# A long convolution by FFT on one Trainium2 core: the first transform stage with the tokens as the stationary operand, evicted by ScalarE

## Chip, cores and metric

The program runs on one core of a Trainium2 chip. The metric is device time in microseconds, the median of several executions. All data are float32. The engines that matter are TensorE (PE in the profile, with its weight loads in a row of their own, PEld), VectorE (DVE), ScalarE (ACT), GpSimd (POOL) and SyncE (SP), which only issues transfers here.

## The reference

Two blocks follow each other. The first convolves every channel of x with a filter as long as the sequence; the second is a soft mixture of experts, in which 32 slots are filled by a softmax over the tokens, pass through small two-layer networks, and are handed back to the tokens by a softmax over the slots.

```python
batch, seq, d_model = (8, 5696, 128)          # x, and h of (seq, d_model)
Xf = np.fft.rfft(x, n=2 * S, axis=1)
Hf = np.fft.rfft(h, n=2 * S, axis=0)
y = np.fft.irfft(Xf * Hf[None], n=2 * S, axis=1)[:, :S, :]
...
x = y.reshape(B * S, D)                       # 45568 x 128
logits = x @ phi                              # phi: 128 x 32
d = exp(logits - logits.max(0)); d /= d.sum(0) + 1e-9
slot_input = d.T @ x                          # 32 x 128
...                                           # 8 experts, 4 slots each
c = exp(logits - logits.max(1)); c /= c.sum(1) + 1e-9
out = c @ slot_out
```

## The kernel before

The transform of 5696 tokens is split into a first stage over 89 rows (90 frequencies, of which 45 pairs are kept) and a second over 64 columns, both as dense matrix products. The 128 channels are taken 64 at a time. I call the work on 64 channels of one sequence a **half**: halves 0 and 1 are the filter h, halves 2 to 17 are the eight sequences of x. `H` counts them.

- `load_x(H)` (L181, issues on L189) brings a half into `X[H % 2]`, 89 rows by 64 tokens by 64 channels, by eight transfers on SP's queue. Two buffers.
- `fold(H, j)` (L192, instructions on L202), j = 0 to 3, on GpSimd: 32 sums and 32 differences of mirrored tokens, written over X. Each j makes a quarter of both, so a product of the first stage needs all four.
- `stage_a(H, k)` (L205), the first stage. The cosine and sine tables `s1` are stationary (89 x 32), X is moving (32 tokens x 16 channels, 512 columns). Eight products fill two PSUM banks `pa`, in which the frequencies lie on the partitions. A VectorE transpose of 32 x 32 blocks (L224) then puts the tokens on the partitions, in `F1` or `F3`. Six such units make a half: four of 64 slots, two of the 26 slots that are left over. `pa` has one buffer, F1 and F3 too.
- `stage_b1(n)` (L231), the second stage (PE, L249, into PSUM `bt`, one buffer), and four VectorE operations: two products with the filter's spectrum (L277; L272 where the form doesn't allow one operation) and two sums (L291). For halves 0 and 1 the products are with phase tables, in four operations, and the sums are the filter's spectrum.
- `stage_b2(n)` (L296): the inverse of the second stage (PE, L310 and L321), a ScalarE eviction (L325, L330) to `zst`, and a transfer to DRAM (`z`, L331, SP's queue).

The main loop (L587) runs over **steps** n; H and i are n divided by 6 and its remainder, and each half takes six steps. In step n the order is: `stage_b1(n)` with its two products, one `stage_a` unit (none at i = 0), the sums, `stage_b2(n - 1)`, a second `stage_a` unit (only at i = 5), `load_x(H + 2)` at i = 3, then a third of the rest of the pipeline, called **C** here, and at i = 5, 0, 1, 2 one `fold`. The unit at i = 3 is the first of half H + 1.

C works from step 26 on, on a quarter of a sequence at a time (32 in all), three steps each. At i = 2 and 5: `stage_c3` (logits), `dispatch` and the first two inverse products of `stage_c1` (PE, L379, from `zc`). At i = 0 and 3: `stage_c6`, `column_max`, `stage_c4` (with the GpSimd subtraction on L460), the last two products of `stage_c1` (L379), their VectorE folds (L385, L386), four GpSimd additions and subtractions (L401), and `load_pair` (L351), which brings the next `zc` from DRAM over SP's queue. At i = 1 and 4: `stage_c5`, `softmax` (GpSimd product on L480) and `stage_c2`, PE transposes of what L401 wrote (L410). `zc` has one buffer here. Where a new sequence begins, `load_pair` runs at i = 1, because the last `z` block must be written first.

The schedule is manual: on each engine the instructions stand in the order in which the code issues them.

Of the kernel before, what the change touches and what calls it, by code (L numbers as in the profile page):

```python
# [23 lines left out]
def slots_of_tail(NG):  # L24

    ks = np.zeros(NG, dtype=int)
    for s in range(NG):
        o, par = divmod(s, 2)
        ks[s] = 2 * (2 * (o // 2) + par) + o % 2 if o < NG // 2 - 1 else NG - 2 + par
    return ks  # L30


def transform_tables(S, N1, N2, CH):

# [4 lines left out]
    NG = N1 - 64  # L39
# [5 lines left out]
    kg = 64 + slots_of_tail(NG)  # L45
    s1 = np.zeros((P, 3, 3, 32))
    s1[:R1, :, 0] = part[:, :, 0:64:2]
    s1[:R1, :, 1] = part[:, :, 1:64:2]
    s1[:R1, :, 2, :NG] = part[:, :, kg]
# [14 lines left out]
    wt = np.zeros((2, N2, 32, N2))  # L64
    wg = np.zeros((2, N2, NG, N2))
    vt = np.zeros((2, N2, 2, 16, N2))
    vg = np.zeros((2, N2, NG // 2, N2))
    t1 = np.zeros((2, N2, 2, 4, 2, 4))
    t3 = np.zeros((2, N2, 2, NG // 2))
    for a in range(2):  # L70
        for s in range(32):
            k = 2 * s + a
            wt[a, :, s] = fore[k]
            o, par = divmod(s, 2)
            vt[par, :, a, o] = w[k][back].T
            t1[par, :, :, o // 4, a, o % 4] = cs[:, k].T
        for s in range(NG):
            wg[a, :, s] = fore[kg[s]]
    for s in range(NG):
        o, par = divmod(s, 2)  # L80
        vg[par, :, o] = w[kg[s]][back].T
        t3[par, :, :, o] = cs[:, kg[s]].T
    wt, wg, vt, vg, t1, t3 = [t.reshape(P, *t.shape[2:]) for t in (wt, wg, vt, vg, t1, t3)]
    return [np.ascontiguousarray(t, dtype=np.float32) for t in (s1, i1, wt, wg, vt, vg, t1, t3)]
# [3 lines left out]
def kernel(  # L88
# [29 lines left out]
    NG = N1 - 64  # L118
    HD = D // 2
    assert S == R1 * N2 and R1 == N1 - 1 and D == P and CH == Q == 4  # L120
# [3 lines left out]
    t_s1, t_i1, t_wt, t_wg, t_vt, t_vg, t_t1, t_t3 = [  # L124
        nc.inline_tensor(t, f"tab_{n}").ap()
        for n, t in zip(("s1", "i1", "wt", "wg", "vt", "vg", "t1", "t3"),
                        transform_tables(S, N1, N2, CH))]
# [35 lines left out]
    s1 = fconst.tile([P, 3, 3, 32], F32, name="s1")  # L163
    wt = fconst.tile([P, 32, N2], F32, name="wt")
    wg = fconst.tile([P, NG, N2], F32, name="wg")
    vt = fconst.tile([P, 2, 16, N2], F32, name="vt")
    vg = fconst.tile([P, NG // 2, N2], F32, name="vg")
    t1 = fconst.tile([P, 2, 4, 2, 4], F32, name="t1")
    t3 = fconst.tile([P, 2, NG // 2], F32, name="t3")
    H1 = [fconst.tile([P, 2, 4, 2, 4, HD], F32, name=f"H1{i}") for i in "ri"]  # L170
    H3A = [fconst.tile([P, 2, 2, 8, 32], F32, name=f"H3A{i}") for i in "ri"]
    H3B = [fconst.tile([P, 2, 2, 5, 32], F32, name=f"H3B{i}") for i in "ri"]
    F1 = bpool.tile([P, 32, 2, HD], F32, name="F1")
    F3 = bpool.tile([P, 32, 2, 32], F32, name="F3")
    X = [apool.tile([P, N2 + 8, HD], F32, name=f"X{i}") for i in range(2)]
# [5 lines left out]
    def load_x(H):  # L181

        if H >= NH:
            return
        g, dh = divmod(H, 2)
        src = (h if g == 0 else x[g - 1]).rearrange("(a n) d -> a n d", n=N2)
        for n0 in (0, 48, 16, 32):
            for r in (slice(0, SPLIT), slice(SPLIT, R1)):
                nc.sync.dma_start(out=X[dh][r, 8 + n0:24 + n0, :],  # L189
                                  in_=src[r, n0:n0 + 16, dh * HD:(dh + 1) * HD])  # L190

    def fold(H, j):  # L192


        if H >= NH:
            return
        t_ = X[H % 2]
        lo = 8 + 8 * j
        hi = 71 - 8 * j
        for op_, dst in ((AL.add, t_[0:R1, 8 * j:8 * j + 8, :]),  # L200
                         (AL.subtract, t_[0:R1, hi:hi - 8:-1, :])):
            nc.gpsimd.tensor_tensor(out=dst, in0=t_[0:R1, lo:lo + 8, :],  # L202
                                    in1=t_[0:R1, hi:hi - 8:-1, :], op=op_)

    def stage_a(H, k):  # L205


        if H >= NH:
            return lambda: None
        t_ = X[H % 2]  # L210
        p = aps.tile([P, 2, 512], F32, name="pa", tag="pa")
        for c in range(2):
            for q in range(4):
                a, comp = divmod(q, 2)
                d0 = 16 * k if k < 4 else 16 * (k - 4) + 32 * a
                nc.tensor.matmul(p[32 * q:32 * q + 32, c, :],  # L216
                                 s1[0:R1, comp + c, a if k < 4 else 2, :],
                                 t_[0:R1, 40 * comp:40 * comp + 32, d0:d0 + 16],
                                 start=True, stop=True)

        def turn():
            f_ = F1[:, :, :, 16 * k:16 * k + 16] if k < 4 else \
                F3[:, :, :, 16 * (k - 4):16 * (k - 4) + 16]
            nc.vector.transpose(f_.rearrange("p k c d -> p c d k"),  # L224
                                p[:, :, :].rearrange("p c (n d) -> p c d n", d=16))

        return turn
# [3 lines left out]
    def stage_b1(n):  # L231


        H, i = divmod(n, 6)
        g, dh = divmod(H, 2)
        bt = bps.tile([P, 2, 512], F32, name="bt", tag="bt")
        o0, no = (0, 4) if i < 4 else (0, 8) if i == 4 else (8, 5)
        for o in range(no):
            for a in range(2):
                r = slice(a * HP, (a + 1) * HP)  # L240
                for par in range(2):
                    if i < 4:
                        s = 8 * i + 2 * o + par
                        l_, m_ = wt[r, s, :], F1[r, s, :, :]
                    else:
                        s = 2 * (o0 + o) + par
                        l_, m_ = wg[r, s, :], F3[r, s, :, :]
                    w_ = 2 * (HD if i < 4 else 32)
                    nc.tensor.matmul(bt[par * HP:(par + 1) * HP, a, o * w_:(o + 1) * w_], l_,  # L249
                                     m_.rearrange("p c d -> p (c d)"), start=True, stop=True)  # L250
        dn = HD if i < 4 else 32
        pi = bpool.tile([P, 2, 512], F32, name="pi", tag="pi")
        y_ = bpool.tile([P, 1024], F32, name="y", tag="y", bufs=2) if g else None

        def split(t):
            return t[:, :, 0:no * 2 * dn].rearrange("p a (o c d) -> p a o c d", c=2, d=dn)

        pv, iv = split(bt), split(pi)
        Hs = [[H1, H3A, H3B][max(0, i - 3)][k][:, dh] for k in range(2)]
        if i < 4:  # L260
            Hs = [v[:, i] for v in Hs]
        if g:
            fs = [[v, v] for v in Hs]
        else:
            fs = [(t1[:, k, i] if i < 4 else
                   t3[:, k, o0:o0 + no].unsqueeze(1).broadcast_to([P, 2, no])).unsqueeze(3)
                  .broadcast_to([P, 2, no, dn]) for k in range(2)]
            fs = [[v, v] for v in fs]
        for dst, f_ in ((iv, fs[1]), (pv, fs[0])):
            if i == 5 or g == 0:  # L270
                for c in range(2):
                    nc.vector.tensor_tensor(out=dst[:, :, :, c, :], in0=pv[:, :, :, c, :],  # L272
                                            in1=f_[c], op=AL.mult)
            else:
                m = lambda v: v.rearrange("p a o c d -> p (a o) c d")
                w_ = f_[0].rearrange("p a o d -> p (a o) d").unsqueeze(2)
                nc.vector.tensor_tensor(out=m(dst), in0=m(pv), in1=w_.broadcast_to([P, 2 * no, 2, dn]),  # L277
                                        op=AL.mult)

        def sums():  # L280
            if g == 0:
                outs = [(0, AL.add, Hs[0]), (1, AL.subtract, Hs[1])]
            else:
                if i < 4:
                    yv = y_[:, :].rearrange("p (a o c d) -> p a o c d", a=2, c=2, d=dn)
                else:
                    yv = y_[:, 0:no * 128].rearrange("p (o c a d) -> p a o c d", c=2, a=2, d=dn)
                outs = [(1, AL.add, yv[:, :, :, 1, :]), (0, AL.subtract, yv[:, :, :, 0, :])]
                prods[n] = y_
            for c, op_, dst in outs:  # L290
                nc.vector.tensor_tensor(out=dst, in0=pv[:, :, :, c, :], in1=iv[:, :, :, 1 - c, :],  # L291
                                        op=op_)
# [3 lines left out]
    def stage_b2(n):  # L296
        H, i = divmod(n, 6)
# [4 lines left out]
        bz = bps.tile([P, 2, 512], F32, name="bz", tag="bz")  # L302
        st = bpool.tile([P, 4, 2, P], F32, name="zst", tag="zst", bufs=2)
        if i < 4:
            for o in range(4):
                for par in range(2):
# [559 lines left out]
```

## Time and profile before

| | |
|---|---|
| median of three runs | 1081.16 us (1080.51 to 1091.31) |
| the profiled execution's own time | 1075.27 us |
| its span | 1073.3 us |
| PE busy, share of the span | 828.1 us, 77% |
| DVE busy | 784.3 us, 73% |
| POOL busy | 408.1 us, 38% |
| ACT busy | 338.0 us, 31% |
| mean granted TensorE clock | 0.888 |

The times of this document are from the profiled execution unless it says otherwise. Groups of instructions are given with their line in the kernel, the tile written and the tiles read, the shape, the number of records and the mean duration of one. A float32 product leaves two records on PE, each with a weight load on PEld. The span falls into a start (to 51 us, the first `stage_b1`), four halves without C (to 254 us), the halves with C (to about 910 us) and a tail without any first stage.

### The profile page before, as it was taken

What the parts mean: (1) busy time and instruction counts of PE and PEld (TensorE: products, weight loads), DVE (VectorE), ACT (ScalarE), POOL (GpSimd) and SP (SyncE); (2) the same over time, 40 slices, a digit from 0 to 9 for tenths busy, and PEclk for the clock granted to TensorE, in tenths of its full rate; (3) what the DMA queues carried; (4) which work ended last, traced back from release to release, by engine and by line L of the source; (5) the groups of instructions that cost most, each with busy time, mean ns of one, the idle gap of its engine ahead of it and who ended that gap; (6) DMA issues with size and microseconds to landing.
All of it is one profiled execution on the core that took longest, in us unless ns stands there. A gap on an engine that the chain in (4) does not pass through costs nothing.

```text
span 1073.3 us, 28430 instructions
## 1 busy us (share of the span) xinstructions
PE 828.1 (77%) x12368; PEld 455.5 (42%) x12368; DVE 784.3 (73%) x1025; ACT 338.0 (31%) x661; POOL 408.1 (38%) x387
## 2 busy tenths in 40 slices
PE   0655557676888888887988888888888888896893
PEld 0122223343444444444544444444444445444683
DVE  1275656666878789888988888898888989484442
ACT  0000001111233334334343343343343434476432
POOL 3402120303234535464654535465453534275000
PEclk9975555867889999999999999999999999896865
DMA  9130301634758574868658384866758345965499
GB/s 228 18 53 3 55 1 40 127 88 108 158 165 166 145 177 126 186 147 210 129 173 191 121 196 132 212 121 192 163 150 177 118 150 186 310 221 226 154 381 340
DMA packets 222040, 167.55 MB, mean 156 GB/s; under 512 B 108438, under 2 KB 204182, under 8 KB 218774
## 3 DMA queue, kind: packets, MB, share of 16 engines
q1 hardware_dynamic: 220620, 162.04, 57.7%
q10 hardware_dynamic: 1296, 3.68, 1.1%
q8 instruction: 98, 1.61, 0.6%
q14 instruction: 26, 0.21, 0.1%
HBM read 90.30 MB, written 75.31 MB: 154 GB/s over the span
## 4 chain that ended last, share of the span: by engine, by line
PE 28%; DVE 26%; DMA 19%; POOL 10%; ACT 3%; issue 3%; SPq 2%; DVEq 0%; POOLq 0%; ACTq 0%
DMA zc<-z 15%; PE pa L216 9%; POOL y L401 8%; DVE F L224 6%; PE bank L379 6%; PE bt L249 6%; DVE y L291 4%; DMA out_dram<-o 4%; DVE pi L277 3%; DVE bt L277 3%; POOL L L460 2%; PE bank L410 2%; DVE y L385 2%; DVE y L386 2%; SPq L189 2%
## 5 line engine op out<-in xcount | busy, mean ns | idle before, releaser
L216 PE MATMUL pa<-X,s 89*32 89x512 f32 x1728 | 248.9, 698 | 51.8 <-POOL X L202 27.4
L224 DVE STREAM_TRANSPOSE F<-pa 128x1024 f32<-128x1024 f32 x108 | 212.2, 1965 | 81.5 <-PE pa L216 81.4
L325 ACT ACTIVATE zst<-bz 128x1024 f32<-128x1024 f32 x96 | 91.6, 955 | 547.7 <-PE bz L310 431.2
L202 POOL TENSOR_TENSOR X<-X 89x512 f32<-89x512 f32 x144 | 183.2, 1273 | 197.7 <-DMA X<-in_x_dram 173.0
L379 PE MATMUL bank<-zc,i 128*64 128x512 f32 x480 | 119.6, 618 | 42.8 <-DMA zc<-z 22.8
L249 PE MATMUL bt<-F,wt 64*64 64x128 f32 x2304 | 94.2, 310 | 56.1 <-DVE y L291 24.2
L249 PEld LDWEIGHTS bt<-F,wt 64*64 64x64 f32 x2304 | 74.4, 152 | 107.4 <-issue 70.0
L216 PEld LDWEIGHTS pa<-X,s 89*32 89x32 f32 x1728 | 49.9, 120 | 162.2 <-issue 94.4
L291 DVE TENSOR_TENSOR y<-bt,pi 128x512 f32<-128x512 f32 x192 | 115.5, 640 | 0.7
L451 POOL MEMSET dt<- 64x8 f32 x32 | 3.4, 108 | 267.2 <-issue 249.8
L277 DVE TENSOR_TENSOR pi<-bt,H1i 128x1024 f32<-128x1024 f32 x64 | 78.0, 1219 | 26.3 <-PE bt L249 26.3
L410 PE MATMUL bank<-ident,y 109*128 109x109 f32 x512 | 67.0, 267 | 33.7 <-ACT d L470 19.0
L401 POOL TENSOR_TENSOR y<-y,op 128x512 f32<-128x512 f32 x64 | 77.4, 1210 | 34.1 <-DVE op L385 31.5
L310 PEld LDWEIGHTS bz<-y,vt 64*64 64x64 f32 x2048 | 58.9, 139 | 56.8 <-issue 56.8
L277 DVE TENSOR_TENSOR bt<-bt,H1r 128x1024 f32<-128x1024 f32 x64 | 78.2, 1222 | 0.0
L310 PE MATMUL bz<-y,vt 64*64 64x128 f32 x2048 | 75.0, 287 | 0.0
L410 PEld LDWEIGHTS bank<-ident,y 109*128 109x128 f32 x512 | 52.5, 145 | 45.8 <-POOL y L401 38.9
L379 PEld LDWEIGHTS bank<-zc,i 128*64 128x64 f32 x480 | 30.5, 138 | 94.5 <-issue 39.0
L401 POOL TENSOR_TENSOR y<-y,om 128x512 f32<-128x512 f32 x56 | 66.7, 1191 | 2.2
L385 DVE TENSOR_TENSOR y<-bank,y 128x512 f32<-128x512 f32 x32 | 22.1, 689 | 60.8 <-PE bank L379 60.8
L249 PE MATMUL bt<-F,wg 64*64 64x64 f32 x1872 | 39.8, 238 | 24.9 <-DVE y L291 11.2
L412 ACT ACTIVATE yt<-bank 128x360 f32<-128x360 f32 x128 | 53.8, 476 | 16.4 <-PE bank L410 16.4
(109 smaller groups left out, 1041.1 us busy)
## 6 DMA issues: line engine op xcount, KB each, us to landing
z<-zst SPq DMA_DIRECT2D x80, 512.0 KB
zc<-z SPq DMA_DIRECT2D x30, 1024.0 KB
X<-in_x_dram SPq DMA_DIRECT2D x64, 320.0 KB
out_dram<-o SPq DMA_DIRECT2D x16, 1024.0 KB
zc<-z SPq DMA_DIRECT2D x30, 416.0 KB
out_dram<-o SPq DMA_DIRECT2D x8, 768.0 KB
z<-zst SPq DMA_DIRECT2D x16, 320.0 KB
c_t<-cst SPq DMA_DIRECT2D x26, 180.0 KB
```

What stands on the lines that cost most here:

```text
L202: nc.gpsimd.tensor_tensor(out=dst, in0=t_[0:R1, lo:lo + 8, :], in1=t_[0:R1, hi:hi - 8:-1, :], op=op_)
L216: nc.tensor.matmul(p[32 * q:32 * q + 32, c, :], s1[0:R1, comp + c, a if k < 4 else 2, :], t_[0:R1, 40 * comp:40 * comp + 32, d0:d0 + 16], ...
L224: nc.vector.transpose(f_.rearrange("p k c d -> p c d k"), p[:, :, :].rearrange("p c (n d) -> p c d n", d=16))
L249: nc.tensor.matmul(bt[par * HP:(par + 1) * HP, a, o * w_:(o + 1) * w_], l_, m_.rearrange("p c d -> p (c d)"), start=True, stop=True)
L277: nc.vector.tensor_tensor(out=m(dst), in0=m(pv), in1=w_.broadcast_to([P, 2 * no, 2, dn]), op=AL.mult)
L291: nc.vector.tensor_tensor(out=dst, in0=pv[:, :, :, c, :], in1=iv[:, :, :, 1 - c, :], op=op_)
L310: nc.tensor.matmul(bz[a * HP:(a + 1) * HP, par, o * P:(o + 1) * P], vt[r, a, 4 * i + o, :], y_[r, k * P:(k + 1) * P], start=True, stop=True)
L325: nc.scalar.activation(st[:, 0:no, :, :].rearrange("p o q x -> p q o x"), bz[:, :, 0:no * P].rearrange("p q (o x) -> p q o x", x=P), AF.Copy)
L379: nc.tensor.matmul(p[h_ * HP:(h_ + 1) * HP, :], i1[0:kr, tab, :], t_[0:kr, h_, o, :, :, q, :].rearrange("k n e d -> k (n e) d"), start=Tru ...
L401: eng.tensor_tensor(out=part_, in0=part(v, 0), in1=o_[:, :, :], op=sign)
L410: nc.tensor.transpose(p[:, i * TR:(i + 1) * TR], ys[T][0:TR, k * CH + i, 0:D], ident[0:TR, 0:TR])
L412: nc.scalar.activation(yt[:, k * CH:(k + 1) * CH, :, :], of_tokens(p), AF.Copy)
```

## The change

The first stage swaps its operands: 32 folded tokens of one channel become the stationary operand, and the tables are moving. Each product then leaves the tokens on the partitions directly. Four products (sums and differences, for even and odd frequencies) go to the four groups of 32 PSUM partitions; 16 channels make 64 products, and one ScalarE activation moves the unit to `Fs`. The 45 slots are cut into 24 and 21, so a half has eight units, l = 0, 1 and k = 0 to 3. Rows of X are padded from 64 to 66 channels. The leftover slots lose their own form: F1 and F3 become `Fs`, and stages b1 and b2 handle six blocks of slots in one way (five of eight slots, one of five).

```diff
-    s1 = fconst.tile([P, 3, 3, 32], F32, name="s1")
...
+    s1 = fconst.tile([P, 2, 2, 3, SL], F32, name="s1")
...
+    SL = 24
     HD = D // 2
+    XP = HD + 2
...
-    X = [apool.tile([P, N2 + 8, HD], F32, name=f"X{i}") for i in range(2)]
+    Fs = bpool.tile([P, NP, 2, HD], F32, name="Fs")
+    X = [apool.tile([P, N2 + 8, XP], F32, name=f"X{i}") for i in range(2)]
...
-    def stage_a(H, k):
...
-        p = aps.tile([P, 2, 512], F32, name="pa", tag="pa")
-        for c in range(2):
-            for q in range(4):
-                a, comp = divmod(q, 2)
-                d0 = 16 * k if k < 4 else 16 * (k - 4) + 32 * a
-                nc.tensor.matmul(p[32 * q:32 * q + 32, c, :],
-                                 s1[0:R1, comp + c, a if k < 4 else 2, :],
-                                 t_[0:R1, 40 * comp:40 * comp + 32, d0:d0 + 16],
-                                 start=True, stop=True)
-        def turn():
-            f_ = F1[:, :, :, 16 * k:16 * k + 16] if k < 4 else \
-                F3[:, :, :, 16 * (k - 4):16 * (k - 4) + 16]
-            nc.vector.transpose(f_.rearrange("p k c d -> p c d k"),
-                                p[:, :, :].rearrange("p c (n d) -> p c d n", d=16))
-        return turn
+    def stage_a(H, l, k):
         t_ = X[H % 2]
+        p = aps.tile([P, 16, HD], F32, name="pa", tag="pa")
+        s0, ns = l * SL, min(SL, NP - l * SL)
+        for d in range(16):
+            for q in range(4):
+                a, comp = divmod(q, 2)
+                nc.tensor.matmul(
+                    p[32 * q:32 * q + 32, d, 0:2 * ns].rearrange("p (c k) -> p c k", c=2),
+                    t_[0:R1, 40 * comp:40 * comp + 32, 16 * k + d],
+                    s1[0:R1, a, l, comp:comp + 2, 0:ns], start=True, stop=True)
+        nc.scalar.activation(
+            Fs[:, s0:s0 + ns, :, 16 * k:16 * k + 16],
+            p[:, :, 0:2 * ns].rearrange("p d (c k) -> p k c d", c=2), AF.Copy)
...
+    for k in range(4):
+        stage_a(0, 0, k)
+    stage_a(0, 1, 0)
     fold(1, 0)
-    for k in range(4):
-        stage_a(0, k)()
+    fold(1, 1)
...
-        turns = [(H + 1, 0)] if i == 3 else [(H + 1, 1)] if i == 4 else \
-            [(H + 1, 2), (H + 1, 3)] if i == 5 else [(H, 3 + i)] if i else []
+        turns = [(H, 1, i + 1)] if i < 3 else []
+        if i >= 2:
+            turns.append((H + 1, 0, i - 2))
+        if i == 5:
+            turns.append((H + 1, 1, 0))
...
-        if i in (5, 0, 1, 2):
-            fold(H + 2 if i == 5 else H + 1, (i + 1) % 6)
+        if i in (4, 5, 0, 1):
+            fold(H + 2 if i >= 4 else H + 1, (i + 2) % 6)
```

In a step the units now stand so: one at i = 0, 1, 3 and 4, two at i = 2 and i = 5, the second of them after `stage_b2`. The first unit of half H + 1 moves from i = 3 to the second place of i = 2, and each `fold` moves one step ahead. The tables and the filter's spectrum are laid out anew to fit; their loads at the start become fewer, of about the same size.

## The prediction

> **What bounds the kernel now.** I read the page first: the two busiest engines and the clock, in 40 slices of 26.8 us.
>
> ```profile
> PE   0655557676888888887988888888888888896893
> DVE  1275656666878789888988888898888989484442
> PEclk9975555867889999999999999999999999896865
> ```
>
> In the first quarter PE and DVE are half busy and the granted clock is low; from slice 12 on both are at eight tenths and the clock is full. Neither is a plain bound. Next the groups that the change touches:
>
> ```profile
> L216 PE MATMUL pa<-X,s 89*32 89x512 f32 x1728 | 248.9, 698 | 51.8 <-POOL X L202 27.4
> L224 DVE STREAM_TRANSPOSE F<-pa 128x1024 f32<-128x1024 f32 x108 | 212.2, 1965 | 81.5 <-PE pa L216 81.4
> ```
>
> The transposes are 212.2 us of DVE, all of which go. What that is worth is read from the order of time. Without C, the trace shows b1, a unit, its transpose, the sums and only then the next b1 (bt has one buffer): halves 0 to 3 start at 51.37, 103.76, 156.34 and 205.73 and end at 253.60, that is 52.4, 52.6, 49.4 and 47.9 us, with a unit at 3.64 us at the low clock and 1.92 at the full one. So there the transpose is on the path.
>
> With C it isn't. PE of one step i = 2 in the timeline (start, length), then GpSimd around it, then SP at the next i = 3:
>
> ```profile
> 604.90 1.10 PE L249 MATMUL bt<-F,wt 64*64 64x128 f32 x32
> 605.93 1.92 PE L216 MATMUL pa<-X,s 89*32 89x512 f32 x16
> 607.79 1.10 PE L310 MATMUL bz<-y,vt 64*64 64x128 f32 x32
> 608.82 0.81 PE L418 MATMUL bank<-yt,phi 128*32 128x360 f32 x8
> 609.45 1.07 PE L491 MATMUL bank<-y,d 128*32 128x129 f32 x32
> 610.86 2.02 PE L379 MATMUL bank<-zc,i 128*64 128x512 f32 x8 [0.34 <-ACT lt L424]
> ```
>
> ```profile
> 599.15 2.46 POOL L401 TENSOR_TENSOR y<-y,op 128x512 f32<-128x512 f32 x2
> 601.56 2.47 POOL L401 TENSOR_TENSOR y<-y,om 128x512 f32<-128x512 f32 x2
> 603.99 2.63 POOL L202 TENSOR_TENSOR X<-X 89x512 f32<-89x512 f32 x2
> 606.58 1.04 POOL L480 TENSOR_TENSOR L<-L,rs 128x512 f32<-128x512 f32 x1
> 607.59 5.32 POOL L202 TENSOR_TENSOR X<-X 89x512 f32<-89x512 f32 x4
> ```
>
> ```profile
> 618.45 8.35 SPq L189 DMA_DIRECT2D X<-in_x_dram  x8
> 627.37 1.10 SPq L359 DMA_DIRECT2D zc<-z  x2
> ```
>
> PE has hardly a gap. L401 ends at 604.03, PE's transposes of it release the next step, and GpSimd still owes folds and L480 until 612.9. At i = 3 SP issues X for 8.35 us ahead of zc, whose product starts 9.2 us after its issue (636.56) and 8.4 a half later. Halves start at 591.21, 638.42 and 686.88: 47.85 us in the mean.
>
> **The change part by part.**
>
> *A unit on PE.* 64 products of 48 or 42 columns replace 8 of 512. No row is that narrow, but single records of 64 columns (64 x 64 stationary) start in fours 58 ns apart, of 128 columns (32-column stationary) 109 ns: 53.3 and 106.7 ns of columns, and 5 or 2 over. I take 45 and 40 ns for a four, 32 fours a unit: 1.44 and 1.28 us, mean 1.36 against 1.85 from start to start; at the low clock 2.7 and 2.5. Eight make 10.9 us a half, six were 11.1. The other bound is the 58 ns row itself: 1.86. In these rows fours of products start 7 ns apart, so issue isn't dearer than 28 ns a four.
>
> One thing no row has: the weight load steps through X by 264 bytes. The Trainium skill, "SBUF — State Buffer", in its specifications and the note on cachelines, says that SBUF has 16-byte lines and that each access in a new line pays; no run here shows it yet. If that doubles a 32-column load to the time of a 64-column one, the unit is 1.86 us and the sum below ends about 28 us higher. "TensorE: Matmul & The Clock Gate" (Wait — 56ns, not 53.3ns?) gives products a floor of about 25 ns from start to start; the 58 ns fours of the trace are 14.5 each, so the measurement decides against it; with it a unit would be 3.2 us and the sum about 100 higher.
>
> *Its eviction on ACT.* L325 takes 1.026 us for 1024 elements and 0.598 for 512, so 0.81 us for 768 if order is free. L537 reads strided at 889 ns for 352 elements, 2.0 ns each or 1.7 us: the far end. L520, which also jumps 64 floats in PSUM, takes 273 for 88 against 244 by the L325 line. Nearest to that: 0.9 us. 144 of them add 130 us to an engine at 31%; when a unit ends it is free (last work of the step before: yt, 0.4 us after PE's transposes). Behind the eviction on ACT stand zst and, at i = 2 and 5, lt; the far end would hold each back by 0.8 us.
>
> *Edits at nothing.* b1 loses 24 products a half (0.1 us). DVE's last block grows from 320 to 384 elements in six operations (0.4 us), behind PE. X already moves in rows of 256 bytes (89 x 64 x 18 = 102,528 of the page's 108,438 packets under 512 bytes), so padding adds none; each us that SP would lose on X is a us of the third piece below, 12 in all. The folds now at i = 4 and 5 wait on GpSimd for X, some 16 us after i = 3 begins; nothing but them is queued there until L460 of the next half, at about 31. If X came 10 us later, L460 would wait too.
>
> *Start.* The last fold ends about 28.7. Before, four units with transposes reach b1 at 51.37. Now five units of 2.6 + 1.0: b1 at 46.7. **-5.**
>
> *Halves 0 and 1.* DVE needs 4.06 us a step (53.42 to 57.50), b1 1.98: 6.28 from b1 to b1 without a unit in the path (51.37 to 57.65). Steps with two units: b1 2.0, unit 2.7, eviction 1.0, unit 2.6: 8.3. A half is 4 x 6.28 + 2 x 8.3 = 41.7 at the low clock, 6 x 5.3 = 31.8 at the full one. I take 40, since the clock there was 0.54 to 0.58: **-25** for both.
>
> *Halves 2 and 3.* At the low clock PE binds: 2.0 + 2.6 + 2.0 = 6.6, or 9.3 with two units: 45 us. At the full clock b1 and DVE (1.04 + 3.73 + 0.25): 30. Take the middle, 37.5, as the clock was 0.7: **-22**. The rest of half 4 before C: **-3.** Front: **-55** (-30 to -80).
>
> *Halves with C,* three pieces of each.
>
> i = 0 and 1: a unit is added at i = 0, ahead of L379, and one at i = 1 gets shorter. The pieces lasted 13.7 and 13.3. GpSimd binds: 6.9 to L460's start as now (591.21 to 598.14; DVE's sums and a reduction come first), L460 1.05, L401 4.93, last transposes 0.95: 13.8. L379's second pair ends 1.4 later, at 7.0, and DVE's fold of it at 7.75, still ahead of L460's end. **+0.3.**
>
> i = 2: the unit that came second-next now stands here and needs all four folds. The last is issued at i = 1, on GpSimd behind L401, another fold and L480. From L401's end, 0.95 before the step: 2.63 + 1.04 + 2.63 puts the folds' end at 5.4, while b2 ends at 3.4. PE waits 2.0 us; behind the wait stand this unit 1.4, c3, dispatch (1.75 together) and L379 (2.0, and 0.2 for lt): 10.7 against 7.9 and 9.2. **+2.1.** Before, this unit stood at 613.85, after the folds' end. This is the change's new wait.
>
> i = 3 to 5: the wait for zc. zst is out 0.5 us earlier (shorter unit, but its eviction ahead): X issue from 5.1, 8.35 long, zc at 14.0, product at 22.8, done 24.7, against 25.6 and 26.0. PE alone would be there at 20.3, so no more is gained. **-1.1.**
>
> Sum +1.35 in each of twelve halves, 5 to 16: **+16.** The last half and the tail keep their time. Net -39: 1075.27 becomes 1036. The profiled execution is 5.9 under the median of the runs, so 1042.
>
> **The rivals.**
>
> *DVE was the bound* (10%): 11.8 us less DVE a half should shorten the halves with C too. For it: DVE at eight or nine tenths. Against: PE is busy 40.7 of the 47 us from 590, and waits 18.6 us for zc between 320 and 900. Were the folds in time and X issued faster, 4 us off each of 12, with -60 in front: about 975.
>
> *It cancels* (17%): units at 1.86 us or evictions at 1.7. In the front about -40; with C three units a half on the path add 0.5 each, so +2.85 x 12 = +34: about 1075 by the runs.
>
> *The strided weight load is much slower* (25%), the case that ends slower. A unit costs the path 3 x 12 with C and some 20 in front, about 55 us per us of unit, so break-even is at 1.36 + 39/55 = 2.1 us, 65 ns a four; slower by 1% from 71 ns. At twice the 58 ns row, 3.7 us, it gives 1042 + 55 x 2.35 = 1171; at 80 ns, 1108. For it: no stationary operand in this trace is strided. Against: L216's moving operand jumps every 16 floats and runs at full rate.
>
> The forecast's own case has 48%.
>
> **How the numbers follow.** One per cent, 11 us, is about what a measurement here can tell from no change. Faster: 48 + 10, less 0.01 for the forecast's upper end: 0.57. Same: 17 and that 0.01: 0.18. Slower: 0.25. The range goes from 1012 (front -80, +10 with C) to 1103, which takes in the cancelling case and the weight load up to some 77 ns a four; left out are the first rival and the dearest tenth of the third.
>
> **What would show it.** L224 gone, and ScalarE's Fs group of 144 near 0.9 us. First b1 near 47; halves 0 to 3 at 40, 40, 38, 38. With C, halves near 49, and at i = 2 PE waiting some 2 us for POOL's X. A four of the new products at 45 ns. It is wrong if fours are over 65 ns, if the halves with C fall under 46, or if halves 2 and 3 stay at 45 at the low clock.

## The result, and the profile after

The changed kernel takes 1244.34 us in the median of four executions (1240.52 to 1245.19). The kernel before, with its further executions, stands at 1084.85. The ratio is 1.146, with a 95% interval of 1.138 to 1.153. The forecast was 1042 and its range ended at 1103: the sign was wrong, and no case in it reached this time through what happened. The profiled execution took 1243.97 us, its span is 1241.9 and its mean granted clock 0.862.

From the page after, in its order: PE, DVE and the clock in 40 slices (31 us each now), the queue row that the prediction passed over, the chain of waits by engine, and the groups of the first stage with their idle time.

```profile
PE   1777787778888887788788888788788888888784
DVE  1355543445454644455555554455546555647442
PEclk9876977888888988888988998898889989788855
...
q8 instruction: 222, 3.64, 1.3%
...
PE 66%; issue 14%; DVE 6%; ACT 5%; POOL 4%; DMA 4%; SPq 0%; DVEq 0%; ACTq 0%; POOLq 0%
...
L192 PE MATMUL pa<-s,X 89*32 89x48 f32 (+1 forms) x18432 | 359.6, 245 | 128.9 <-issue 97.0
L192 PEld LDWEIGHTS pa<-s,X 89*32 89x32 f32 x18432 | 332.7, 164 | 165.1 <-issue 131.6
L196 ACT ACTIVATE Fs<-pa 128x768 f32<-128x768 f32 (+1 forms) x144 | 111.0, 771 | 557.2 <-PE pa L192 557.2
```

The same row of the page before:

```profile
q8 instruction: 98, 1.61, 0.6%
```

DVE has fallen from eight or nine tenths to four or five, and the eviction takes 0.77 us. But PE's time is not work alone. "issue", time in which an engine waits for nothing that the profile shows, is 14% of the chain, and it stands in front of L192. Queue 8, the one that the page calls "instruction", moved 222 packets of 16.4 KB where it had moved 98.

What such a wait looks like, in PE's timeline of the step at 614.23 (i = 2; start, length, and in brackets the idle time before):

```profile
614.23 1.10 PE L214 MATMUL bt<-Fs,wt 64*64 64x128 f32 x32
615.26 2.27 PE L192 MATMUL pa<-s,X 89*32 89x42 f32 x128
617.46 1.10 PE L259 MATMUL bz<-y,vt 64*64 64x128 f32 x32
618.49 0.33 PE L192 MATMUL pa<-s,X 89*32 89x48 f32 x2
622.29 2.71 PE L192 MATMUL pa<-s,X 89*32 89x48 f32 x123 [3.48 <-issue]
```

The second unit stops after two or three records for 3.48 us and then runs on: its operands, its bank and its weights were there. GpSimd's folds, which the prediction made this unit wait for, had ended a microsecond before it began:

```profile
614.22 1.05 POOL L416 TENSOR_TENSOR L<-L,rs 128x512 f32<-128x512 f32 x1 [0.46 <-DVE rs L415]
615.23 2.28 POOL L181 TENSOR_TENSOR X<-X 89x512 f32<-89x512 f32 x2
```

I put all of PE's records in one row: 28,208 of products, 28,208 of weight loads and 374 of its sequencer (semaphores and drains) that stand between them. In 70 places one record starts over 1.2 us after the last, and 46 of these lie at the same place of a 256-record grid. One packet of queue 8 corresponds to 256 such records (56,790 in 222 packets), and a unit, 128 records of products and 128 weight loads, is just such a block. I call the change from one block to the next a crossing, and the times of over 0.4 us from one record's start to the next one's at that place the gaps at the blocks' ends. They add up to 162.8 us, of which PE is idle for 137.7. The trace before has 0.9 us at the same place of the grid, and 11.1 at the place where most of its own gaps of over 1.2 us stand. In the case above a packet starts at 619.41, lands at 620.75, and PE runs again at 622.08. Over the trace PE resumes 1.43 us after a landing (1.28 to 1.60 in the middle eight tenths). From one packet's start to the next it is 3.27 us at the least, 3.73 at the first quartile and 4.29 in the median; before, the least was 4.64 and the median 9.53. A whole unit took 2.93 us in the mean from its first record's start to its last one's, 2.15 in the median.

The time by stages, from the first b1 of each half, with the forecast and two of the experiments below (us):

| | before | forecast | after | half the products | sums first to step 26 |
|---|---|---|---|---|---|
| start | 51.4 | 46.7 | 42.7 | 43.3 | 51.0 |
| halves 0, 1 | 52.4, 52.6 | 40, 40 | 42.1, 41.0 | 40.2, 41.0 | 43.9, 44.4 |
| halves 2, 3 | 49.4, 47.9 | 37.5, 37.5 | 42.2, 44.8 | 34.0, 32.6 | 39.7, 40.0 |
| half 4 | 51.1 | 48.1 | 62.1 | 53.7 | 52.0 |
| one half of 5 to 16 | 47.75 | 49.1 | 63.9 | 50.4 | 47.7 |
| what follows | 195.6 | 195.6 | 200.8 | 196.7 | 195.9 |

After minus forecast: -4 at the start, +15 in halves 0 to 3, +14 in half 4, 12 x 14.8 = +177 in the halves with C, +5 at the end, together 207.

Pauses of PE also go with a low clock, which the PEclk rows hint at: in halves 5 to 16 the granted clock stood at half for 150 of the 766 us, against 2 of 573 in the kernel before. All 24 stretches at half clock begin 1.2 to 4.6 us after the start of a pause of PE at a crossing (pauses of 1.5 to 6.2 us), none more than 1.2 us after its end. The gaps at the blocks' ends are 117 us in these halves. How their 177 us divide between gaps and clock was not parted, since pauses that make up 64 of the 117 us end inside the stretches at half clock.

### The profile page after: what moved, and what is told of

Read it like the earlier page. It is cut to its first block, busy times and chain, and to the rows that moved or that the text cites. A ratio compares the mean times of both kernels' runs of the same rounds, so it can differ in the third digit from the quotient of the medians.

```text
span 1241.9 us, 60157 instructions
## 1 busy us (share of the span) xinstructions
PE 980.8 (79%) x28208; PEld 762.9 (61%) x28208; DVE 616.5 (50%) x917; ACT 445.9 (36%) x789; POOL 383.8 (31%) x387
## 3 DMA queue, kind: packets, MB, share of 16 engines
q8 instruction: 222, 3.64, 1.3%
## 4 chain that ended last, share of the span: by engine, by line
PE 66%; issue 14%; DVE 6%; ACT 5%; POOL 4%; DMA 4%; SPq 0%; DVEq 0%; ACTq 0%; POOLq 0%
PE pa L192 25%; PE bt L214 10%; PE bank L315 9%; PE bz L259 8%; PE bank L346 4%; POOL y L337 3%; PE op L754 2%; PE bank L427 2%; PE bank L354 2%; DMA out_dram<-o 2%; POOL X L181 1%; DMA X<-in_h_dram 1%; PE bank L403 1%; ACT lt L360 1%; ACT cst L461 1%
## 5 line engine op out<-in xcount | busy, mean ns | idle before, releaser
L192 PE MATMUL pa<-s,X 89*32 89x48 f32 (+1 forms) x18432 | 359.6, 245 | 128.9 <-issue 97.0
L192 PEld LDWEIGHTS pa<-s,X 89*32 89x32 f32 x18432 | 332.7, 164 | 165.1 <-issue 131.6
L196 ACT ACTIVATE Fs<-pa 128x768 f32<-128x768 f32 (+1 forms) x144 | 111.0, 771 | 557.2 <-PE pa L192 557.2
L181 POOL TENSOR_TENSOR X<-X 89x512 f32<-89x512 f32 x144 | 157.4, 1094 | 168.3 <-DMA X<-in_x_dram 145.5
L214 PEld LDWEIGHTS bt<-Fs,wt 64*64 64x64 f32 x3312 | 105.6, 150 | 71.3 <-issue 42.5
L214 PE MATMUL bt<-Fs,wt 64*64 64x128 f32 x3312 | 135.0, 305 | 17.8 <-DVE Hr L239 10.7
L259 PE MATMUL bz<-y,vt 64*64 64x128 f32 x2880 | 123.5, 304 | 26.5 <-issue 26.4
L226 DVE TENSOR_TENSOR pi<-bt,Hi 128x1024 f32<-128x1024 f32 x80 | 97.5, 1218 | 69.0 <-PE bt L214 69.0
L259 PEld LDWEIGHTS bz<-y,vt 64*64 64x64 f32 x2880 | 93.9, 149 | 36.6 <-issue 31.2
L226 DVE TENSOR_TENSOR bt<-bt,Hr 128x1024 f32<-128x1024 f32 x80 | 97.8, 1222 | 0.0
L346 PEld LDWEIGHTS bank<-ident,y 109*128 109x128 f32 x512 | 62.0, 165 | 43.4 <-POOL y L337 21.5
```

The costliest lines, as they stand in the source:

```text
L181: nc.gpsimd.tensor_tensor(out=dst, in0=t_[0:R1, lo:lo + 8, 0:HD], in1=t_[0:R1, hi:hi - 8:-1, 0:HD], op=op_)
L192: nc.tensor.matmul(p[32 * q:32 * q + 32, d, 0:2 * ns].rearrange("p (c k) -> p c k", c=2), t_[0:R1, 40 * comp:40 * comp + 32, 16 * k + d], ...
L196: nc.scalar.activation(Fs[:, s0:s0 + ns, :, 16 * k:16 * k + 16], p[:, :, 0:2 * ns].rearrange("p d (c k) -> p k c d", c=2), AF.Copy)
L214: nc.tensor.matmul(bt[par * HP:(par + 1) * HP, a, o, :, :].rearrange("p c d -> p (c d)"), wt[r, s, :], Fs[r, s, :, :].rearrange("p c d -> ...
L226: nc.vector.tensor_tensor(out=m(dst), in0=m(bt), in1=w_.broadcast_to([P, 8, 2, HD]), op=AL.mult)
L259: nc.tensor.matmul(bz[a * HP:(a + 1) * HP, par, o, :], vt[r, a, 4 * u + o, :], y_[r, a, o, :, :].rearrange("p c d -> p (c d)"), start=True ...
```

## The experiments

The seven runs on the new stage's cost (up to the one without padding) are one execution each. The theory, A: TensorE's instructions do not come fast enough. The rival, B: the new products themselves are dear, the strided weight load above all (the prediction's own third rival).

**The weight load made contiguous.** 32 channels of one token instead of 32 tokens of one channel, so the numbers are others.

```diff
-                    t_[0:R1, 40 * comp:40 * comp + 32, 16 * k + d],
+                    t_[0:R1, 40 * comp + d, 0:32],
```

> The kernel after, but the stationary operand of each first-stage product is 32 neighbouring channels of one token (contiguous) in place of 32 tokens of one channel (264 bytes apart). The products are then of other numbers; their count, shapes and columns are the same. Theory A (TensorE waits for its instructions, which arrive in blocks of 16 KB): the products may get faster, but each block still takes some 3.4 us to come, so the waits at block boundaries grow by what the products gain: 1220 to 1244 us. Theory B (the strided weight load is what costs): a four of products falls from 63 to 45 ns, a unit by 0.6 us, and 144 units on the path give some 85 us: about 1160 us.

1235.47 us, 9 less (this run, and the half-count, eight-times and no-padding runs below, had a kernel before of 1076.13 beside them). In the groups of its page (busy, mean of one, idle before) the records get shorter and the idle time longer:

```profile
L192 PE MATMUL pa<-s,X 89*32 89x48 f32 (+1 forms) x18432 | 287.1, 228 | 155.6 <-issue 122.7
L192 PEld LDWEIGHTS pa<-s,X 89*32 89x32 f32 x18432 | 256.9, 129 | 196.9 <-issue 162.5
```

A four takes 43 ns in the median, against 65 in the changed kernel, and a weight load 110 against 163. So the strided load does cost 20 ns a four. But of the 72.5 us of busy time that PE saves in L192 hardly any is won: the gaps at the blocks' ends grow from 162.8 to 211.9 us. The time is in A's range, and the strided load falls as the main cause of the loss.

**Half the products, same columns.** Each product streams its tables twice, for two channels; every second channel gets its neighbour's transform.

```diff
-        for d in range(16):
+        for d in range(0, 16, 2):
...
-                    p[32 * q:32 * q + 32, d, 0:2 * ns].rearrange("p (c k) -> p c k", c=2),
+                    p[32 * q:32 * q + 32, d:d + 2, 0:2 * ns].rearrange("p d (c k) -> p d c k", c=2),
...
-                    s1[0:R1, a, l, comp:comp + 2, 0:ns], start=True, stop=True)
+                    s1[0:R1, a, l, comp:comp + 2, 0:ns].unsqueeze(1).broadcast_to([R1, 2, 2, ns]),
+                    start=True, stop=True)
```

> The kernel after with 32 products of 96 or 84 columns a unit instead of 64 of 48 or 42: the tables stream twice past each stationary operand, so every second channel gets its neighbour's transform. Columns are the same, instructions of the first stage half (TensorE's per half of 64 channels from about 3200 to 2200, 8.6 blocks of 256 instead of 12.6). Theory A: the waits of TensorE at block boundaries all but vanish; 1244 falls to 1050 to 1090 us. Theory B: the strided loads halve too, a unit falls to about 1.4 us and 144 units give some 90 us, but waits without a releaser stay: about 1150 us.

1048.53 us, 196 less than the changed kernel, with the same columns on PE, the same order and the same eviction:

```profile
q8 instruction: 150, 2.46, 1.0%
...
L192 PE MATMUL pa<-s,X 89*32 89x96 f32 (+1 forms) x9216 | 248.6, 262 | 52.5 <-POOL X L181 32.4
L192 PEld LDWEIGHTS pa<-s,X 89*32 89x32 f32 x9216 | 216.2, 145 | 85.2 <-issue 38.2
```

"issue" is no longer the main releaser of L192's products, and the time is just below A's range. The gaps at the blocks' ends are 37.8 us, 125 less, and L192's busy time falls by 111 us. A unit takes 1.31 us in the median, and fours take 82 and 74 ns, the 80 and 70 of their columns. But this run halves the weight loads too, so B was not quite out. Two more runs part them.

**The same, with tiny products added.** Ahead of every product of that run one with 2 x 2 columns.

```diff
+                nc.tensor.matmul(p[32 * q:32 * q + 2, d, 0:2], t_[0:R1, 40 * comp, 0:2],
+                                 s1[0:R1, a, l, comp, 0:2], start=True, stop=True)
```

> The unit of the half-count run (32 products of 96 or 84 columns, every second channel with its neighbour's transform), and ahead of each of them a tiny product: 2 of X's tokens as a stationary operand of 2 columns, 2 table columns moving, written where the real product then writes. TensorE gets as many instructions as the changed kernel, 18432 products in this stage, but the added ones carry a twenty-fourth of the columns and hardly any weights. Theory A (the supply of PE's instructions limits, blocks of 256 records at 3.3 us or more each): about 221 blocks again and 1200 to 1250 us, with PE's gaps ending at every 256th record. Theory B (what the products do on PE, their columns and weights, limits, and the half-count run was faster because it has fewer weight loads of 32 strided columns): 1048 plus 9216 starts of some 7 to 11 ns, 65 to 100 us less what hides, 1080 to 1130 us, and few gaps at the blocks' ends.

1256.49 us, 208 more than without them and just above A's range, with 161.2 us of gaps at the blocks' ends. Its page:

```profile
PE 981.2 (78%) x28208; PEld 750.2 (60%) x28208; DVE 616.6 (49%) x917; ACT 445.2 (35%) x789; POOL 383.2 (31%) x387
...
q8 instruction: 221, 3.62, 1.3%
...
L194 PE MATMUL pa<-s,X 89*32 89x96 f32 (+1 forms) x9216 | 363.5, 281 | 43.1 <-issue 36.0
L192 PE MATMUL pa<-s,X 89*2 89x2 f32 x9216 | 294.8, 170 | 80.8 <-issue 54.7
```

With products added that do next to nothing (L192 here), the kernel is as slow as the changed one. The number of instructions decides here, not what they do. PE's "busy" is 981.2 us against the changed kernel's 980.8, for a quite different mix: a busy PE is here one whose instructions trickle in.

**The same half count, weight load contiguous.** The edits of the first two runs together.

> The half-count unit with the stationary operand read contiguously (32 channels of one token in place of 32 tokens of one channel, so the numbers are others). 150 blocks as in the half-count run. If the strided weight load costs anything once instructions come in time, the fours of 96 columns fall below 82 ns and the time goes under 1040. If it is hidden behind the columns: fours at 80 to 83 ns and 1043 to 1052 us, the same as the half-count run.

1038.27 us beside a kernel before of 1084.09 (the half-count run had 1076.13 beside it). Fours take 82 and 74 ns as with the stride, so on PE the load hides behind the columns, as the second expectation had it; the time meets the first. Halves 5 to 16 differ by 0.4 us each. With one execution of each, these 10 us are not settled; more than that the strided load does not cost here.

**The kernel before, with eight times the products.** Theory A must hold for other code too: each product of 512 columns is cut into eight of 64.

```diff
+            for e in range(0, 16, 2):
...
-                nc.tensor.matmul(p[32 * q:32 * q + 32, c, :],
...
-                                 t_[0:R1, 40 * comp:40 * comp + 32, d0:d0 + 16],
+                        t_[0:R1, 40 * comp:40 * comp + 32, d0 + e:d0 + e + 2],
```

> The kernel before with each product of 512 columns cut into eight of 64 (32 tokens x 2 channels), same stationary tables, contiguous: 64 products a unit as in the kernel after, the same columns in all, the same output. TensorE's instructions per half rise from about 1460 to 2800, 11 blocks. Theory A: waits at block boundaries appear, and 1081 us becomes 1130 to 1220. Theory B: no strided load, fours of 64 columns take 58 ns as they do elsewhere, a unit keeps its 1.85 us: 1075 to 1090 us.

1321.51 us with 192 packets and 101.1 us of gaps at the blocks' ends. It was slower than A said, and DVE's busy time went from 784 to 945.8 us, POOL's from 408 to 496: something else was in it.

**The same with X's rows padded to 66 channels,** as in the changed kernel.

```diff
-    X = [apool.tile([P, N2 + 8, HD], F32, name=f"X{i}") for i in range(2)]
+    X = [apool.tile([P, N2 + 8, HD + 2], F32, name=f"X{i}") for i in range(2)]
```

> The eight-times kernel (before, 64 products of 64 columns a unit) with rows of X padded to 66 channels, because there the fours took 97 ns in place of 58 and VectorE and GpSimd got slower too, which points to the 256-byte step of its moving operand. Theory A (instruction blocks): fours near 58 ns, VectorE and GpSimd back to 784 and about 400 us, but some 190 blocks of instructions and waits at their boundaries of 100 us or more: 1130 to 1220 us. Theory B (array and SBUF alone): with the 256-byte step gone it is as fast as the kernel before: 1075 to 1090 us.

1277.72 us. DVE is back at 795.6 and POOL at 382.7; the gaps are 145.8 us, and L192's picture appears on the old first stage:

```profile
L217 PE MATMUL pa<-X,s 89*32 89x64 f32 x13824 | 299.3, 253 | 124.4 <-issue 82.5
```

The sign is A's, the size not: 197 us more than before, beyond the 1220 at which A's estimate ended. Here each unit's wait also holds up a transpose and with it DVE (a unit takes 3.3 us in the mean from its first record's start to its last one's), which the estimate left out.

**The changed kernel without its padding.**

```diff
-    XP = HD + 2
+    XP = HD
```

> The kernel after with rows of X of 64 channels instead of 66 (stationary operand 256 bytes apart). Theory A: no change within 1%, 1232 to 1256 us. Theory B: if the step matters by its alignment, fours go well above 64 ns and the time by some 55 us per us of unit; if only by leaving the 16-byte line, nothing changes.

1443.02 us, and the surprise of the study: not only do weight loads take 246 ns and fours 121. VectorE and GpSimd slow down too, even on instructions that have nothing to do with X, such as L322. First two groups of the changed kernel (busy time, mean), then this run's page:

```profile
L181 POOL TENSOR_TENSOR X<-X 89x512 f32<-89x512 f32 x144 | 157.4, 1094 | 168.3 <-DMA X<-in_x_dram 145.5 <-DMA X<-in_h_dram 14.8
...
L322 DVE TENSOR_TENSOR y<-bank,y 128x512 f32<-128x512 f32 x32 | 22.1, 691 | 1.1
```

```profile
PE 1199.4 (83%) x28208; PEld 990.9 (69%) x28208; DVE 994.9 (69%) x917; ACT 507.4 (35%) x789; POOL 652.4 (45%) x387
...
L181 POOL TENSOR_TENSOR X<-X 89x512 f32<-89x512 f32 x144 | 329.8, 2290 | 182.1 <-DMA X<-in_x_dram 158.6
...
L322 DVE TENSOR_TENSOR y<-bank,y 128x512 f32<-128x512 f32 x32 | 106.1, 3317 | 1.1
```

What the slowed operations collide with can be read from the order in time: of the 64 operations of L322 the 12 beside which no L192 runs still take 691 ns, the 52 beside L192 4.07 us in the median. In the changed kernel both kinds take 691.

The gaps at the blocks' ends shrink to 58.0 us, as fits a PE that now works more slowly than its instructions come. Neither expectation held: A expected no change, and B's rate of 55 us per us of unit makes about 100 us of fours that went from 65 to 121 ns, where 199 came.

**Only the order.** The prediction's front gain came from taking the transpose out of the way between b1 and the sums. That needs no new stage: in the kernel before, the sums are issued ahead of the transpose.

```diff
-        if turns:
-            stage_a(*turns.pop(0))()
+        turn = stage_a(*turns.pop(0)) if turns else lambda: None
         sums()
+        turn()
```

> The kernel before with one change: VectorE's two sums are issued ahead of the transposes of the same step, so the next second-stage products, which wait for the sums, no longer wait for a transpose. If the transpose was on the path in the halves without C, as the prediction had it, those four halves lose some 1.3 us a step (24 steps): about 1045 to 1055 us; with C nothing is gained. If it was not on the path: 1081.

1062.13 us, ratio 0.984 (0.978 to 0.990). That is short of the 1045 to 1055 expected. Halves 0 to 3 fall to 43.9, 43.4, 38.3 and 38.2, 38 us less in all; halves 5 to 16 get 2.4 us longer each, 29 in all. Moving `load_x` behind `load_pair` on SP as well was to win those back:

> As sums first, and load_x moved behind load_pair in the step i = 3, so that the transfers of zc are issued ahead of X's eight. If the wait for zc at i = 5 set the length of the halves with C, 12 halves lose 1 to 2 us more than with sums first alone: 15 to 25 us below it. If PE's own order sets it, no more than 5 us.

1066.36 us, ratio 0.987 (0.982 to 0.992): it does not. With X padded besides:

> As the one before, with rows of X padded to 66 channels. If the 256-byte step disturbs VectorE and GpSimd also where the moving operand reads 16 channels at a time, folds and VectorE operations get shorter and a few us go; if not, no change within 0.5%.

1058.53 us, ratio 0.980 (0.976 to 0.985); the intervals of the three overlap, so no difference among them is shown. So the new order was confined to where it gains, with `if n < 26` for the late transpose and the old place from step 26 on:

> The kernel before, with the sums issued ahead of the transpose in steps 0 to 25 only (before C begins); from step 26 on the old order. If the gain of that order lies in the front and its loss in the halves with C: halves 0 to 3 at 44, 43, 38 and 38 us as in the run with the sums first throughout, against 52, 53, 49 and 48, and the halves with C at 47.8 again, against 50.1: 1081 - 39 + 3 for half 4 = about 1045 us, ratio 0.965. If the 2.4 us that the halves with C lost follow from the earlier start of the work instead (transfers that fall otherwise), they stay at 50 and the time near 1062.

1040.46 us, ratio 0.966 (0.960 to 0.971), the fastest kernel of the study that computes the reference, and the gain stands where it should: 34 of the 38 us in halves 0 to 3, and the halves with C at 47.7 again. Its timeline in half 0 (PE's b1 and unit, DVE's sums and transpose):

```profile
57.24 1.99 PE L249 MATMUL bt<-F,wt 64*64 64x128 f32 x32 [4.29 <-DVE H1i L291]
...
59.16 3.02 PE L216 MATMUL pa<-X,s 89*32 89x512 f32 x16
...
62.07 0.69 DVE L291 TENSOR_TENSOR H1r<-bt,pi 128x512 f32<-128x512 f32 x1
62.68 0.68 DVE L291 TENSOR_TENSOR H1i<-bt,pi 128x512 f32<-128x512 f32 x1
63.28 1.94 DVE L224 STREAM_TRANSPOSE F<-pa 128x1024 f32<-128x1024 f32 x1
...
63.51 1.10 PE L249 MATMUL bt<-F,wt 64*64 64x128 f32 x32 [1.34 <-DVE H1i L291]
```

The transpose now runs beside the next b1. b1 follows b1 after 6.27 us (57.24 to 63.51), the 6.28 of the prediction's step without a transpose. Where the halves with C lost their 2.4 us when the sums came first, the trace of that run shows. At i = 5 the second unit waits for the late transpose of the first, in each half for 1.95 us where it was 1.05 before:

```profile
309.66 1.91 DVE L224 STREAM_TRANSPOSE F<-pa 128x1024 f32<-128x1024 f32 x1
...
311.63 2.85 PE L216 MATMUL pa<-X,s 89*32 89x512 f32 x16 [1.97 <-DVE F L224]
```

Nine of these twelve pauses, and two for zc, come with a stretch at half the granted clock that begins in the pause or at most 1.6 us after it. Halves 5 to 16 spend 54 us at half clock there, against 2 in the kernel before and 2 in the run with the old order from step 26 on. In these stretches PE starts 15.9 records a us, against 28.5 in the rest of these halves; by these rates they cost some 24 of the 29 us, an estimate.

Padding X on top of the confined order gives nothing more:

> The same with rows of X padded from 64 to 66 channels, the changed kernel's own layout, and nothing else. Folds on GpSimd at 1091 ns against 1274 (144 of them, 0.7 us a fold step). If they set the wait at i = 0 with C, 6.9 us to the subtraction on L460 and what follows, up to 0.7 us a half less: another 5 to 10 us, 1035 to 1042. If not, 1045 as without it.

1043.9 us, ratio 0.969 (0.963 to 0.975), though GpSimd's folds fall from 1272 to 1093 ns: they do not set the end there.

## Why the prediction was wrong

The step that failed is the price of a unit on PE, 1.36 us, and in it the sentence "In these rows fours of products start 7 ns apart, so issue isn't dearer than 28 ns a four". It took the pace inside a burst for a pace that can last. In the trace before, a dense burst such as b1 was 32 records with 32 weight loads in 1.03 us, 16 ns each, a block of 256 in 4.1 us; and packets on queue 8 never started less than 4.64 us apart. The forecast's unit asks for a whole block in 1.36 us. The trace after shows 3.27 us at the least for a block, and the unit took 2.93 us in the mean. So eight units of a half want 8 x 3.3 = 26 us of supply where the forecast gave them 10.9 of PE, and unless other, slower work stands between two units (b1, b2, L379), PE waits. The row `q8 instruction: 98, 1.61, 0.6%` was on the page before, and the change adds 124 blocks; it was neither costed nor made a rival.

By runs: halving the instructions took 196 us off, adding nearly empty ones put 208 on, and taking the strided load out gave 9. The low clock after PE's pauses was not in the forecast either.

- *Fours at 45 and 40 ns.* About right for contiguous weights (43 in the median). With the stride of 264 bytes a load takes 163 ns instead of 110 and a four 65, just on the bound at which the prediction said it would be wrong, and by its own sum the break-even. By the prediction's rate that would have cost about 40 us had the supply kept up, an estimate. As it was, removing it gave 9, and 10 with the instructions halved.
- *The third rival,* the strided load as the cause of slowness, had the right sign by luck: its 1108 us wanted fours at 80 ns, they were 65, and 1244 us came by another way.
- *Evictions at 0.9 us:* 0.77 measured; PE waited for one only seven times, 6.6 us in all.
- *Start:* first b1 at 42.7 rather than 46.7. The units stood 3.73 us apart, near the 3.6 of the sum, but the first started in earnest at 25.4 and not at 28.7: the first fold began 1.9 us earlier, and the folds of the padded X take 1.09 us instead of 1.27.
- *Halves 0 and 1:* 42.1 and 41.0 against 40. With a mean clock of 0.73 and 0.71 the gaps at the blocks' ends are only 4.5 and 3.0 us. (The 4.06 us of DVE in that sum is 4.08 by the two times beside it; nothing hangs on it.)
- *Halves 2 and 3:* 42.2 and 44.8 against 37.5. With half the instructions they take 34.0 and 32.6, near the end of the prediction's span that it put at 30 and well under its middle. In the changed kernel the clock was 0.90 and 0.77 there, higher than in halves 0 and 1, and the gaps at the blocks' ends 8.5 and 9.7 us: PE wants its instructions faster, and they don't come.
- *With C:* 63.9 against 49.1. The half-count run has 50.4, 1.3 from the forecast, though its way there differs: at i = 2 the wait for the folds was to be 2.0 us in each half, and that run shows 6.9 us in ten waits for them in all after the start, none over 0.8. In the changed kernel nearly all folds are done in time. The waits for zc remain (30.3 us there, 22.8 before). So 50.4 is close to 49.1 in part by luck.
- *The sum:* with the instructions halved, 1048.5 against the 1042 predicted, and each stage within 6 us a half. So what the change does to DVE, ACT and the order was costed about rightly in sum, with misses that in part cancel (-8 us in halves 2 and 3, +6 in half 4, +16 in halves 5 to 16); the supply of its instructions was not costed at all.
- *"Transposes on the path without C, not with it":* right, and the order runs show it: 34 us in halves 0 to 3 by moving one operation behind another, and nothing gained by the same move where C runs.

The Trainium skill, "Runtime: NRT & Kernel Launch" (Instruction fetch mechanics), would have given the size of a block: 16 KiB, 256 instructions, as the packets of queue 8 show (3.64 MB in 222). It goes on that a crossing is "mostly hidden", since engines issue more slowly than blocks arrive, and that PE's memory holds 2048 instructions. This trace says otherwise: 162.8 us of gaps at the blocks' ends. And the next packet starts in the median 1.15 us after a crossing, so PE seems to have about one block ahead of it. After the 42 crossings at which the sixteen DMA engines were over 70% busy for the next 0.6 us, it started 2.8 us later in the median, against 1.0 after the 123 with under 5%. In the case at 618 the packet left 3.6 us after the crossing at 615.81. The load of the sixteen engines from 617 to 623 in forty slices (nine tenths until 617.9), and the two queues in it:

```profile
DMA  9999990900004044530000008999999999300000
...
q1 hardware_dynamic: 1092, 0.97, 62.9%
q8 instruction: 1, 0.02, 1.4%
```

Whether that traffic delayed it was not tried.

## What to carry to other kernels

When a change replaces few long products by many short ones, count TensorE's instructions, weight loads included, and divide by 256: here a stretch that needed a block in less than some 3.3 to 3.7 us waited for its instructions, whatever the products cost, and PE looked busy meanwhile. Read queue 8's row and look for "issue" in front of the new group. And before a stage is rebuilt to take an operation off a path, try whether moving that operation behind its neighbour does the same: here it gave 3.4%, in a few lines. Then read the PEclk row: a longer pause of PE can cost more than its own length.

## What the runs showed of the hardware

- Instructions in blocks of 256 records, at least 3.27 us from one to the next (3.24 in the run without padding), and PE running 1.43 us after a block has landed.
- After most pauses of PE of over 2 us, and some shorter ones, the granted clock was half for 3.4 to 10.2 us: after 23 of 24 in halves 5 to 16 of the changed kernel (150 of 766 us at half clock); pauses of 1.05 us in the kernel before had none after them.
- A stationary operand of 32 columns loads in 110 ns when contiguous, in 163 ns at a step of 264 bytes (139 in the half-count run), and in 246 ns at 256 bytes. At 256 VectorE's and GpSimd's own instructions stretch as well (L322 from 691 to 3317 ns, folds from 1094 to 2290), while ScalarE's eviction stays (773 against 771). The Trainium skill, "SBUF — State Buffer" (Who interferes with whom), names one place of contention, the port pair that VectorE and GpSimd share; these two runs differ only in the padding of X, and with it in the step at which TensorE reads, and show one more, since L322 stretches only beside L192. Which part of the memory is shared was not tried.
- Fours of products with 32-column operands at 43 ns, 10.8 a product, run well under the 25 ns floor that "TensorE: Matmul & The Clock Gate" states (Wait — 56ns, not 53.3ns?), as the 58 ns fours of the trace before already did.
